# A kernel of top-k attention and two expert layers: three early expert blocks, small slots in two pieces, new priorities

## The chip, the cores and the metric

One core of a Trainium2 chip runs the whole program. The metric is the device time in microseconds of one execution. The core has five engines with a queue each: TensorE (PE; PEld is its weight load), VectorE (DVE), ScalarE (ACT), GpSimd (POOL) and SyncE (SP). Each works its queue strictly in the order in which the kernel wrote it. SyncE issues nearly all transfers, GpSimd the indirect ones.

## What is computed

Three stages follow one another. Sizes are 4 sequences of 576 tokens, 8 heads of 64, model width 512, so 2304 tokens in 18 tiles of 128.

```python
def _attn_ref(q, k, v):
    scores = scale * np.matmul(q, k.transpose(0, 1, 3, 2))
    kth = np.partition(scores, -top_k, axis=-1)[..., -top_k:-top_k + 1]   # top_k = 32
    scores = np.where(scores >= kth, scores, -1000000000.0)
    ...
    return np.matmul(attn, v)                                            # softmax over what is left

def _moe_ref(x, mu_k, mu_r, w_k, w_v, w_r):
    xk = mu_k * x + (1.0 - mu_k) * x_prev                                # x_prev: the token before
    xr = mu_r * x + (1.0 - mu_r) * x_prev
    k = np.maximum(xk @ w_k, 0.0)
    return 1.0 / (1.0 + np.exp(-(xr @ w_r))) * (k * k @ w_v)

def _moe2_ref(x, w_gate, w_local, w1, w2):                               # 8 experts, 512 -> 1024 -> 512
    for b in range(B):
        for s in range(S):
            fresh_e = int(np.argmax(logits[b, s]))
            e = fresh_e if s == 0 or local_gate[b, s] < 0.5 else prev_e
            ...
            out[b, s] = p[e] * (np.maximum(x[b, s] @ w1[e], 0.0) @ w2[e])
```

The layer in the middle has weights in 64-bit floats, which the kernel turns into 32-bit ones itself.

## The kernel before

**A planner writes the order.** Every piece of work is an `Op` of a class `Sched`: its engine, an assumed duration, what it depends on, the buffers it takes and gives back, and a priority. `Sched.run` plays the program through on these assumptions; whenever an engine is free, it takes the ready piece with the lowest priority number, and the order so found is the order of each engine's queue. To the priority that the code gives, `op` adds for each kind of work (engine and function name, as `PE minis.l1_`) a `SHIFT` and, times the number of the instance, a `SLOPE`. These tables hold about 85 kinds. The order is fixed at build time; on the chip an engine waits where its next instruction's input is late.

**Attention.** A pair (`pair`) is two heads on one tile of 128 tokens; there are 72. TensorE makes scores (L502, two heads at once on halves of the array), ScalarE copies them out (L508), VectorE finds the 32nd largest (L513 to L556), ScalarE and GpSimd mask and exponentiate (L549 to L567), TensorE transposes (L590) and multiplies with the values (L603). `keys` loads two heads' keys with four transfers (L416, L417, two for each head) into the one buffer `kn`, then TensorE transposes them (L429); `vals` loads values with four transfers (L454, L455) into five buffers; `queries` loads a tile's queries (L463).

**Middle layer.** `narrow` converts the 64-bit weights in 20 pieces (L674 to L708), from the start on. `moe` takes one or two tiles: L801 for the gate, L819 and L866 for the first product, L853 and L894 for the second, L911 and L918 for the routing's logits (L921 stores them). Its result goes to DRAM (`xd`, L905).

**Expert layer.** Tokens are gathered by expert into slots. A block "D" is 256 tokens of one expert, "S" 128, "T" 128 + 32; the small slots "T", "H", "Q" of `minis` have 32, 64 and 32 tokens. Routing (`Routing`, recorded at L1342) runs twice: early, on the first 14 tiles, which fills `KE` blocks "D" and no others, and late, on all 18, which places the rest in the fixed list `MAIN`. If a case doesn't fit the list, a general fallback runs instead. For each block `slots` loads the expert's two weight matrices (L1692, L1694; 4 MB, left out on the chip when the expert is the same as that of the block before; `kept` tells the planner where that is), splits each weight into a high and a low part (L1730 to L1735) since the product is made in three passes, gathers the tokens (L1754), transposes them (L1768), multiplies (L1792 for D and T in pieces of 12 matmuls, L1802 for S; then L1844 in pieces of 3), and scatters the result (L1312). `minis` does the same for the small slots with unsplit weights, several column groups of the array side by side (L1894 for the first product, one piece of work for each of its 4 chunks; L1910 for the second, one for each of its 8).

At the start `Sched` may fill TensorE's planned idle time with a dummy product (L1970).

Of the kernel before, what the change touches and what calls it, by code (L numbers as in the profile page):

```python
# [30 lines left out]
class Op:  # L31
    __slots__ = ("eng", "dur", "fn", "prio", "lat", "port", "mode", "new", "use", "left", "after", "ready", "end", "seq")


class Sched:


    def __init__(self, slots):

        self.cross = {"PE": 0.24, "DVE": 0.15, "ACT": 0.2, "POOL": 0.2, "SP": 0.1}  # L40
        self.same = {"PE": 0.2, "DVE": 0.1, "ACT": 0.14, "POOL": 0.14, "SP": 0.05}
        self.rel = 0.2
        self.shift, self.slope, self.scale, self.port, self.nth = {}, {}, {}, (), {}
        self.tiled, self.turn = {}, 0.1
        self.fill, self.fill_until, self.fill_dur, self.fill_tag = None, 0.0, 0.0, None
        self.free, self.loose = dict(slots), ("pb",)
        self.ops, self.count = [], {}
# [6 lines left out]
    def op(self, eng, dur, fn, deps=(), prio=0.0, new=(), use=(), lat=0.0):  # L54
        o = Op()
# [6 lines left out]
        o.mode = self.tiled.get(key, 0)  # L62
# [16 lines left out]
    def run(self):  # L79
        heads = {t: 0 for t in self.count}  # L80
# [71 lines left out]
def kernel(  # L152
# [32 lines left out]
    KE, MAIN, FULL = 2, ("DTDDDSDT", "THQTQ"), ("D" * (MB // 2) + "S" * E, "")  # L185
# [23 lines left out]
    def segs(t):  # L209
        r = []  # L210
        g = t * P
        while g < (t + 1) * P:
# [40 lines left out]
    SHIFT = {"ACT Routing.own.<lambda>": 90.83780998, "ACT keys.hi": 22.43589903, "ACT minis.fin": 1303.658946,  # L253
             "ACT minis.hev": 979.6428999, "ACT minis.rl": 274.4842701, "ACT minis.xev": -142.1804519,
             "ACT moe.ev": -371.3097322, "ACT moe.hi": 97.84617022, "ACT moe.rc": -247.9308573,
             "ACT moe.rl": 931.2484429, "ACT moe.sq": -422.5721012, "ACT narrow.hi_": -1052.938037,
             "ACT narrow.lo_": -354.1839001, "ACT narrow.o1": -255.7834887, "ACT narrow.o4b": 107.1696191,
             "ACT pair.cp": -25.34393383, "ACT pair.ev": 234.8737767, "ACT pair.ex": 630.9371884,
             "ACT pair.rl": 26.80759231, "ACT queries.hi": -127.4905844, "ACT slots.fin": -546.850338,
             "ACT slots.rl": -434.7448111, "ACT slots.thi": -335.8746519, "ACT slots.xhi": -1731.134606,  # L260
             "ACT split.hi": 1730.558906, "ACT x0_t.cs": -120.4848861, "ACT x0_t.ev": -14.27743458,
             "DVE Routing.__init__.<lambda>": 241.5412186, "DVE Routing.own.<lambda>": 252.5861327,
             "DVE Routing.place.<lambda>": 728.2549627, "DVE Routing.place.counts": 109.1720779,
             "DVE Routing.place.kinds_": 143.1441866, "DVE Routing.place.order": -146.0024522,
             "DVE Routing.place.rows": -481.6913385, "DVE Routing.place.spread": 402.3734509,
             "DVE Routing.place.tokens": -291.9940417, "DVE mix.o1": -745.2170327, "DVE mix.o2": -3353.422116,
             "DVE moe.lc": 245.0135023, "DVE moe.lo": 19.61633349, "DVE moe.xs": 357.0877612,
             "DVE narrow.o1b": -3467.233295, "DVE narrow.o2": 10.77865981, "DVE narrow.o3": 107.1405205,
             "DVE narrow.o4": 69.48365636, "DVE pair.cands": 4660.150012, "DVE pair.ch": -1353.776995,
             "DVE pair.cn": 666.4389245, "DVE pair.rx": 335.8208771, "DVE pair.th": 30.41966953,  # L270
             "DVE slots.tlo": 371.3560689, "DVE slots.xlo": -738.9035906, "DVE split.hi": 146.281663,
             "DVE split.lo": -62.01978119, "DVE kernel.ok_in": -545.3444415,
             "DVE kernel.ok_out": 95.76363139, "DVE x0_t.nrm": 1170.307626,
# [9 lines left out]
             "POOL Routing.place.<lambda>": 1917.782127, "POOL Routing.pool.consts_": 384.2200777,  # L283
             "POOL minis.gx": 351.200011, "POOL minis.sca": -202.5550864, "POOL moe.lo": 270.4878608,
             "POOL narrow.o5": 294.3819007, "POOL narrow.o5r": -298.0169726, "POOL narrow.o6": -218.326335,
             "POOL pair.nbias": 330.3710576, "POOL pair.rp": 1118.836428, "POOL pair.sp": 344.3683001,
             "POOL slots.gx": -13.98307362, "POOL slots.sca": 2858.354949, "POOL slots.tlo": -1495.820284,
             "POOL split.lo": -55.4064238, "POOL x0_t.edge": 731.5562647, "SP dma.keys": 53.35405016,
             "SP dma.queries": 14.05631517, "SP dma.raw": -1463.806281, "SP dma.small": -580.7447585,
             "SP dma.vals": -13.48047754, "SP load.go": -241.494936, "SP minis.first": 216.1179133,  # L290
             "SP minis.second": 63.77269869, "SP moe.<lambda>": 159.110049}
    SLOPE = {"ACT Routing.own.<lambda>": -1801.45762, "ACT keys.hi": 39.07940011, "ACT minis.fin": -1014.9097,
             "ACT minis.hev": 179.643281, "ACT minis.rl": -1270.934339, "ACT minis.xev": -724.8108089,
             "ACT moe.ev": 51.08183119, "ACT moe.hi": -2.29375714, "ACT moe.rc": -391.9016438,
             "ACT moe.rl": 2.954213622, "ACT moe.sq": 0.3153912355, "ACT narrow.hi_": 333.5405295,
             "ACT narrow.lo_": 990.6602289, "ACT narrow.o1": -20.67716147, "ACT narrow.o4b": -212.1268198,
             "ACT pair.cp": 1.994825142, "ACT pair.ev": -12.3860511, "ACT pair.ex": -1.136550945,
             "ACT pair.rl": 1.000926306, "ACT queries.hi": -73.7324358, "ACT slots.fin": -139.4746212,
             "ACT slots.rl": -108.2117739, "ACT slots.thi": 81.23765684, "ACT slots.xhi": 197.2386647,
             "ACT split.hi": -15.53815153, "ACT x0_t.cs": 98.06339663, "ACT x0_t.ev": -96.9242885,  # L300
             "DVE Routing.__init__.<lambda>": -5188.178896, "DVE Routing.own.<lambda>": -187.5434498,
             "DVE Routing.place.<lambda>": -33.26916612, "DVE Routing.place.counts": -1080.433612,
             "DVE Routing.place.kinds_": 1193.087661, "DVE Routing.place.order": 3085.767142,
             "DVE Routing.place.rows": -56.97482649, "DVE Routing.place.spread": 3802.902318,
             "DVE Routing.place.tokens": 181.9509213, "DVE mix.o1": -416.5312326, "DVE mix.o2": 83.38990822,
             "DVE moe.lc": 63.71582267, "DVE moe.lo": -148.0939769, "DVE moe.xs": 44.39229292,
             "DVE narrow.o1b": -8.868595585, "DVE narrow.o2": -420.7801735, "DVE narrow.o3": -245.3131375,
             "DVE narrow.o4": -45.31025859, "DVE pair.cands": -30.9391742, "DVE pair.ch": 26.82931159,
             "DVE pair.cn": 11.27550151, "DVE pair.rx": 2.99460654, "DVE pair.th": -8.218142381,
             "DVE slots.tlo": -181.6041827, "DVE slots.xlo": 283.5184965, "DVE split.hi": -49.03847711,  # L310
             "DVE split.lo": 23.23497517, "DVE kernel.ok_in": -1237.21353,
# [97 lines left out]
    def keys(b, hp, prio):  # L409
# [11 lines left out]
        for j0, nj in ((0, KJ), (KJ, 1)):  # L421
# [11 lines left out]
            def hi(pt=pt, j0=j0, w=w):  # L433
                nc.scalar.activation(kt.t[:, j0 * P:j0 * P + w], pt.t[:, :w], AF.Copy)
# [1425 lines left out]
    def minis(sc2, new, seq, T0):  # L1860
        for kind, s, je, rr_ in seq:
# [62 lines left out]
            for c in range(DC):  # L1924
                def l1_(c=c, l1=l1):
                    l1(c)
# [102 lines left out]
```

## Time and profile before

| | us |
|---|---|
| median of 3 runs | 1012.39 |
| lowest, highest | 1008.04, 1016.09 |
| the profiled execution | 1008.81 |
| its span, first to last instruction | 1007.0 |
| TensorE busy in it | 960.4 |
| VectorE busy | 803.6 |
| mean granted TensorE clock | 0.980 |

The profile's page gives busy shares of each engine over the span, the chain of work that ended last, and the costliest groups of instructions by source line. The trace behind it is asked by stretches of time (how busy each engine was in each), by waits (who waited for whom), and as a timeline. A matmul's end is modelled, so a busy TensorE may still be slower than it could be; the starts of successive pieces tell that.

### The profile page before, as it was taken

To read this page: it belongs to the slowest core of one execution; us is meant where nothing else is said; L and a number is where in the kernel's file an instruction comes from. 1 tells how busy PE (TensorE), PEld (TensorE's weight loads), DVE (VectorE), ACT (ScalarE), POOL (GpSimd) and SP (SyncE) were. 2 spreads that over 40 slices of the span, in tenths; PEclk is the share of its full clock that TensorE was granted. 3 is DMA by queue.
4 is the path that set the end of the run, shared out by engine and by line. 5 is a ranking of instruction groups with operands and counts; after the bars stand their busy time and mean duration, and the time that the engine had idled before them with its cause. 6 is when DMAs were issued, how large, how long until landed. Compare 5 with 4: busy or idle time off the path is not lost.

```text
span 1007.0 us, 22941 instructions
## 1 busy us (share of the span) xinstructions
PE 960.4 (95%) x7498; PEld 717.6 (71%) x7498; DVE 803.6 (80%) x3362; ACT 717.5 (71%) x1661; POOL 715.9 (71%) x836
## 2 busy tenths in 40 slices
PE   7889999999999999999999999999989998999995
PEld 6666666667676777777777777778677875867763
DVE  4869999998998999999768999966589775663651
ACT  5568888999896899898987988973453564544532
POOL 3658888889897899989777979973446645653531
PEclk9899999999998999999999999999899999999998
DMA  7542000121010131010010000000832999737651
GB/s 199 148 152 85 12 12 12 24 69 39 10 33 11 24 82 27 20 34 11 16 54 24 23 22 2 13 11 22 283 116 70 366 298 358 256 137 273 213 180 38
DMA packets 80596, 95.08 MB, mean 94 GB/s; under 512 B 45101, under 2 KB 49197, under 8 KB 80464
## 3 DMA queue, kind: packets, MB, share of 16 engines
q1 hardware_dynamic: 77392, 83.93, 26.3%
q0 software_dynamic: 3072, 9.57, 2.7%
q8 instruction: 61, 1.00, 0.4%
q14 instruction: 71, 0.58, 0.2%
HBM read 84.04 MB, written 9.57 MB: 93 GB/s over the span
## 4 chain that ended last, share of the span: by engine, by line
PE 55%; DVE 22%; ACT 6%; issue 5%; DMA 5%; POOL 4%; SPq 2%; DVEq 0%; POOLq 0%; ACTq 0%
PE pb L1792 7%; PE pb L502 6%; PE pv L1844 6%; PE pv L894 5%; PE pb L866 5%; PE xa L603 5%; DVE c L513 5%; PE pb L590 4%; PE pb L801 4%; DVE c L553 3%; DVE mk L544 3%; POOL mk L549 2%; DVE c L522 2%; DVE c L525 2%; PE pv L853 1%
## 5 line engine op out<-in xcount | busy, mean ns | idle before, releaser
L563 POOL TENSOR_TENSOR at<-s,at 128x576 f32<-128x576 f32 x144 | 204.1, 1427 | 26.8 <-ACT at L559 26.0
L549 POOL TENSOR_TENSOR mk<-s,mk 128x576 f32<-128x576 f32 x144 | 205.5, 1427 | 0.0
L513 DVE MAX8 c<-s 128x8 f32<-128x82 f32 (+1 forms) x1008 | 158.9, 229 | 14.9 <-ACT s L508 14.9
L502 PE MATMUL pb<-kT,qh 64*128 64x288 f32 x640 | 122.6, 460 | 7.3 <-ACT wv L708 3.2
L559 ACT ACTIVATE at<-s,TS 128x576 f32<-128x576 f32 x144 | 111.7, 777 | 22.5 <-DVE TS L556 19.0
L553 DVE MAX8 c<-mk 128x8 f32<-128x584 f32 x144 | 108.0, 756 | 19.9 <-POOL mk L549 19.9
L508 ACT ACTIVATE s<-pb 128x288 f32<-128x288 f32 (+1 forms) x320 | 115.5, 413 | 10.2 <-PE pb L502 9.1
L567 ACT ACTIVATE at<-at,sm 128x576 f32<-128x576 f32 x144 | 112.1, 780 | 12.3 <-POOL at L563 11.8
L544 DVE TENSOR_SCALAR_CACHE_REDUCE mk<-s,c 128x576 f32<-128x576 f32 x144 | 114.2, 800 | 0.0
L593 ACT ACTIVATE aT<-pb 128x384 f32<-128x384 f32 x216 | 97.2, 493 | 10.1 <-PE pb L590 9.1
L590 PE MATMUL pb<-ident,at 128*128 128x128 f32 x648 | 99.4, 282 | 4.3 <-ACT at L567 4.3
L590 PEld LDWEIGHTS pb<-ident,at 128*128 128x128 f32 x648 | 74.3, 143 | 33.5 <-ACT at L567 11.9
L894 PE MATMUL pv<-wv,kk 128*128 128x512 f32 x336 | 98.0, 417 | 0.0
L603 PE MATMUL xa<-aT,vb 128*64 128x128 f32 (+1 forms) x1600 | 94.9, 267 | 0.7 <-ACT aT L593 0.7
L603 PEld LDWEIGHTS xa<-aT,vb 128*64 128x64 f32 x1600 | 78.8, 137 | 21.3 <-issue 17.7
L866 PE MATMUL pb<-xk,wk 128*128 128x256 f32 x672 | 93.7, 291 | 0.1
L1792 PE MATMUL pb<-xk,wk 128*128 128x256 f32 x672 | 89.8, 285 | 2.0 <-DVE xk L1774 2.0
L1792 PEld LDWEIGHTS pb<-xk,wk 128*128 128x128 f32 x672 | 84.2, 188 | 9.1 <-issue 5.1
L866 PEld LDWEIGHTS pb<-xk,wk 128*128 128x128 f32 x672 | 84.9, 191 | 8.0 <-issue 2.8
L1844 PE MATMUL pv<-wv,vb 128*128 128x512 f32 x300 | 83.5, 407 | 0.0
L502 PEld LDWEIGHTS pb<-kT,qh 64*128 64x128 f32 x640 | 52.9, 189 | 40.3 <-issue 11.7
L1735 DVE TENSOR_TENSOR wk<-s,wk 128x512 fp32r<-128x512 f32 x51 | 55.7, 1114 | 28.9 <-ACT wk L1732 25.2
(266 smaller groups left out, 1955.4 us busy)
## 6 DMA issues: line engine op xcount, KB each, us to landing
s<-in_moe_w_dram SPq DMA_DIRECT2D x64, 256.0 KB, 4.7
kT<-in_moe_w_dram SPq DMA_DIRECT2D x32, 512.0 KB, 6.3
rw<-in_moe_w_dram SPq DMA_DIRECT2D x15, 512.0 KB, 6.9
at<-in_moe_w_dram SPq DMA_DIRECT2D x10, 512.0 KB, 4.8
kk<-in_moe_w_dram SPq DMA_DIRECT2D x20, 256.0 KB, 4.4
xd<-rr SPq DMA_DIRECT2D x18, 256.0 KB, 2.0
rw<-in_moe_w_k_dram SPq DMA_DIRECT2D x8, 512.0 KB, 4.6
qn<-in_q_dram SPq DMA_DIRECT2D x16, 256.0 KB, 3.0
```

What stands on the lines that cost most here:

```text
L502: nc.tensor.matmul(pcs[a].t[:, :HS], qh.t[r, hp, :], kt.t[r, c], start=True, stop=True)
L513: nc.vector.max(c8.t[:, a, c, :], s2.t[:, EDGE[c]:EDGE[c + 1]])
L544: nc.vector.tensor_scalar(mk.t[:, :S], s2.t, c8.t[:, a, NCH + 2, 7:8], 0.0, op0=OP.is_lt, op1=OP.add, accum_out=sm.t[:, 2 + a:3 + a])
L549: nc.gpsimd.tensor_tensor(mk.t[:, :S], s2.t, mk.t[:, :S], op=OP.mult)
L553: nc.vector.max(c8.t[:, a, 0, :], mk.t)
L563: nc.gpsimd.tensor_tensor(x, s2.t, x, op=OP.subtract)
L590: nc.tensor.transpose(pt.t[:, c * P:(c + 1) * P], at.t[:, (g * GB + c) * P:(g * GB + c + 1) * P], ident)
L603: nc.tensor.matmul(xa.t[a * D:(a + 1) * D, hp * P + p0:hp * P + p0 + n], vb[:, a, j, :], evs[c // GB][1].t[:, c % GB, p0:p0 + n], start=(j ...
L866: nc.tensor.matmul(pm.t[:, :N], WK[c][f // 4].t[:, x, f % 4 * P:(f % 4 + 1) * P], xk.t[:, y, c, :N], start=(m == 0), stop=(m == 3 * DC - 1))
L894: nc.tensor.matmul(pvs[ti].t, kk.t[:, x, ti * P:(ti + 1) * P], WV[f].t[:, y, :], start=(f == 0 and m == 0), stop=(f == FB - 1 and m == 2))
L1792: nc.tensor.matmul(ph.t[:, (f % 2) * N:(f % 2 + 1) * N], w[:, x], xt.t[:, y, c, :N], start=(n == 0), stop=(n == 3 * DC - 1))
L1844: nc.tensor.matmul(py.t, hT.t[:, x, o_:o_ + P], w[0].t[:, y, :], start=(f == 0 and m == 0), stop=(f == FC - 1 and m == 2))
```

## The change

It has four parts.

- `KE` is 3, not 2: the early routing fills three blocks "D". The late list has one "D" less. `kept` names the place in the list where the planner counts on no load; the last "T" no longer stands there. `b3`, the planned begin of the small slots after the blocks' begin, goes from 30 to 44.
- The small slots' two products are one piece of work each for the planner, not 4 and 8. The matmuls are the same.
- Keys are loaded with two transfers, each for both heads, not four; the planner's duration for it is halved. Loads, transposes and copies of the first sequence's keys, of its values, and those of the first queries count as kinds of their own (`keys0`, `vals0`, `queries0`, `tr0`, `hi0`).
- All `SHIFT` and `SLOPE` values are new, and two tables are added, `EARLY` and `LATE`: with m instances of a kind and h = m / 9, the n-th one's priority gets EARLY times 0.5 to the power n / h and LATE times 0.5 to the power (m - 1 - n) / h.

```diff
     def run(self):
+        for o in self.ops:
+            m = self.nth[o.key] + 1
+            h = m / 9.0
+            o.prio = o.prio + self.early.get(o.key, 0.0) * 0.5 ** (o.nth / h) + self.late.get(o.key, 0.0) * 0.5 ** ((m - 1 - o.nth) / h)
         heads = {t: 0 for t in self.count}
...
-    KE, MAIN, FULL = 2, ("DTDDDSDT", "THQTQ"), ("D" * (MB // 2) + "S" * E, "")
+    KE, MAIN, FULL = 3, ("DTDDDST", "THQTQ"), ("D" * (MB // 2) + "S" * E, "")
...
-    SHIFT = {"ACT Routing.own.<lambda>": 90.83780998, "ACT keys.hi": 22.43589903, "ACT minis.fin": 1303.658946,
...
+             "SP dma.keys": -102.4317918, "SP dma.keys0": 56.14849309, "SP dma.queries": -498.1475508,
+             "SP dma.queries0": 10.45413052, "SP dma.raw": -431.7345715, "SP dma.small": -231.7248161,
+             "SP dma.vals": 37.16374137, "SP dma.vals0": 237.2049297, "SP load.go": 106.8085623,
...
+    SLOPE = {"ACT Routing.own.<lambda>": -1610.984326, "ACT keys.hi": 21.21187526, "ACT keys.hi0": -283.5194928,
...
+             "SP dma.keys": -253.3733908, "SP dma.keys0": 1340.092052, "SP dma.queries": -34.78187054,
+             "SP dma.queries0": -1367.670809, "SP dma.raw": 131.9486322, "SP dma.small": 7669.235697,
+             "SP dma.vals": -75.45162534, "SP dma.vals0": 130.9723499, "SP load.go": 40.97117659,
...
+    EARLY = {"ACT Routing.own.<lambda>": 39.01644115, "ACT keys.hi": -284.7349795, "ACT keys.hi0": -87.75660058,
...
+             "SP dma.keys0": -64.50886934, "SP dma.queries": 126.7084932, "SP dma.queries0": 388.3107358,
...
+             "SP dma.vals0": 124.8441309, "SP load.go": 64.45799412, "SP minis.first": -708.6716305,
...
+    LATE = {"ACT Routing.own.<lambda>": -25.40150862, "ACT keys.hi": 19.0748765, "ACT keys.hi0": 99.36181289,
...
+            "SP dma.keys": 165.7459533, "SP dma.keys0": -239.0713462, "SP dma.queries": 403.0473361,
+            "SP dma.queries0": 274.283792, "SP dma.raw": 0.3699409712, "SP dma.small": -5.4936241,
+            "SP dma.vals": 420.1723432, "SP dma.vals0": -7.891970257, "SP load.go": -547.0614982,
...
-            for h in range(2):
-                e.dma_start(x[:REM, :, h, :], kk_[h, :cut].rearrange("(p j) d -> p j d", j=KJ + 1))
-                e.dma_start(x[REM:, :KJ, h, :], kk_[h, cut:].rearrange("(p j) d -> p j d", j=KJ))
-        ld = dma([go], 2.2, prio - PAR["ka"], [kn], kind="keys")
+            e.dma_start(x[:REM], kk_[:, :cut].rearrange("h (p j) d -> p j h d", j=KJ + 1))
+            e.dma_start(x[REM:, :KJ], kk_[:, cut:].rearrange("h (p j) d -> p j h d", j=KJ))
+        ld = dma([go], 1.1, prio - PAR["ka"], [kn], kind="keys" if b else "keys0")
...
-          "hp": [0, 1, 2], "ps": [0.15, 1.1], "ld": 6.2, "kept": (5, 7), "ts": [12.0, 13.7], "b2": 1650, "w0": [-20, -26],
-          "w1": [-11.5, 4.5], "g": -9.5, "l0": -61, "l1": [-14, -20], "xt": 1, "rl": 300, "l3": -40, "t3": 24.0, "b3": 30.0}
+          "hp": [0, 1, 2], "ps": [0.15, 1.1], "ld": 6.2, "kept": (5,), "ts": [12.0, 13.7], "b2": 1650, "w0": [-20, -26],
+          "w1": [-11.5, 4.5], "g": -9.5, "l0": -61, "l1": [-14, -20], "xt": 1, "rl": 300, "l3": -40, "t3": 24.0, "b3": 44.0}
...
-            for c in range(DC):
-                def l1_(c=c, l1=l1):
+
+            def l1_(l1=l1):
+                for c in range(DC):
                     l1(c)
-                o = sc2.op("PE", 2.0 * F_ / 1200, l1_, [lds[0], xo, o], T0 + 1 + 0.9 * c, [] if c else [ph, h], [xt, W1[c]] + ([ph] if c else []))
+            o = sc2.op("PE", DC * 2.0 * F_ / 1200, l1_, [lds[0], xo], T0 + 1, [ph, h], [xt, *W1])
...
-            for f in range(FC):
-                def l2_(f=f, l2=l2):
+
+            def l2_(l2=l2):
+                for f in range(FC):
                     l2(f)
-                o = sc2.op("PE", 2.0 * D_ / 1200, l2_, [lds[1], ho, o], T0 + 6 + 0.45 * f, [] if f else [py, yo],
-                           [hT, W2[max(f - 1, 0)]] + ([py] if f else []))
+            o = sc2.op("PE", FC * 2.0 * D_ / 1200, l2_, [lds[1], ho], T0 + 6, [py, yo], [hT, *W2])
```

## Rows read from the trace of the kernel before

**Rows 1.** The page's first part: busy us, share of the span, instructions.

```profile
PE 960.4 (95%) x7498; PEld 717.6 (71%) x7498; DVE 803.6 (80%) x3362; ACT 717.5 (71%) x1661; POOL 715.9 (71%) x836
```

**Rows 2.** Table of stages: stretch, length, busy us by engine, clock, DMA share, GB/s.

```profile
0.00:75.00 75.00, 63.08 (x625) 47.86 (x626) 46.73 (x166) 43.88 (x91) 37.36 (x49) 0.91 0.60 168
...
130.00:475.00 345.00, 341.22 (x2723) 246.17 (x2722) 332.31 (x1678) 303.88 (x742) 306.12 (x362) 0.99 0.11 29
475.00:696.00 221.00, 220.54 (x1757) 167.21 (x1756) 178.43 (x888) 179.91 (x437) 178.68 (x242) 1.00 0.08 21
...
735.00:773.00 38.00, 33.29 (x237) 29.17 (x236) 34.24 (x108) 16.66 (x34) 18.80 (x21) 1.00 0.19 68
773.00:838.00 65.00, 59.48 (x390) 46.89 (x386) 49.05 (x87) 35.24 (x73) 37.23 (x35) 0.99 0.94 325
...
901.00:996.00 95.00, 93.95 (x699) 64.59 (x702) 42.89 (x64) 42.23 (x89) 37.34 (x33) 1.00 0.54 183
```

**Rows 3.** TensorE's timeline in the tail: start, us, line, operands, count.

```profile
788.86 0.64 PE L1894 MATMUL pb<-rw,aT 128*32 128x256 f32 x8
...
832.40 0.64 PE L1910 MATMUL pb<-at,qh 128*32 128x128 f32 x16
832.97 0.50 PE L1844 MATMUL pv<-wv,x0T 128*128 128x512 f32 x1
...
842.15 0.42 PE L1910 MATMUL pb<-kk,qh 128*32 128x128 f32 x8
...
844.13 0.43 PE L1910 MATMUL pb<-kk,qh 128*32 128x128 f32 x8
...
994.32 0.43 PE L1910 MATMUL pb<-kk,qh 128*32 128x128 f32 x8
...
995.58 0.43 PE L1910 MATMUL pb<-kk,qh 128*32 128x128 f32 x8
```

**Rows 4.** The chain that ended last, in order of time: start, us, what.

```profile
403.28 1.44 PE pb L866 x12
...
453.16 1.63 PE pb L866 x12
...
866.06 5.76 PE pb L1792 x48
...
916.41 5.74 PE pv L1844 x24
```

**Rows 5.** The page's transfers: out<-in, queue, count, size, median us to landing.

```profile
s<-in_moe_w_dram SPq DMA_DIRECT2D x64, 256.0 KB, 4.7
```

**Rows 6.** SyncE's timeline in the tail.

```profile
737.58 3.16 SPq L1694 DMA_DIRECT2D kT<-in_moe_w_dram  x4
775.29 4.49 SPq L1692 DMA_DIRECT2D s<-in_moe_w_dram  x6
```

**Rows 7.** TensorE's waits, 735 to 838 us: total us, times, longest.

```profile
PE pv L1844 <- DVE wv L1735: 3.2, 1, 3.2
PE pb L1342 <- DVE at L1342: 2.1, 2, 1.6
PE pb L1342 <- DVE mk L1342: 1.2, 1, 1.2
PE pb L1342 <- DVE qn L1342: 1.2, 1, 1.2
```

**Rows 8.** SyncE's timeline at the start.

```profile
25.27 0.60 SPq L455 DMA_DIRECT2D vb<-in_v_dram  x1
...
26.59 0.55 SPq L416 DMA_DIRECT2D kn<-in_k_dram  x1
```

**Rows 9.** VectorE's waits, 0 to 75 us.

```profile
DVE xT L677 <- ACT xT L674: 25.5, 12, 4.4
```

**Rows 10.** TensorE's timeline at 310 us.

```profile
312.63 1.33 PE L502 MATMUL pb<-kT,qh 64*128 64x288 f32 x2 [2.45 <-DVE LG L921]
313.88 2.93 PE L866 MATMUL pb<-xk,wk 128*128 128x256 f32 x12
```

More of the change, by code (lines that the diff above doesn't have):

```diff
@@ L31 @@
 class Op:
-    __slots__ = ("eng", "dur", "fn", "prio", "lat", "port", "mode", "new", "use", "left", "after", "ready", "end", "seq")
+    __slots__ = ("eng", "dur", "fn", "prio", "lat", "port", "mode", "new", "use", "left", "after", "ready", "end", "seq", "key", "nth")
 class Sched:
@@ L43, in __init__ @@
         self.shift, self.slope, self.scale, self.port, self.nth = {}, {}, {}, (), {}
-        self.tiled, self.turn = {}, 0.1
+        self.tiled, self.turn, self.early, self.late = {}, 0.1, {}, {}
         self.fill, self.fill_until, self.fill_dur, self.fill_tag = None, 0.0, 0.0, None
@@ L61, in op @@
         o.port = eng == "POOL" or key in self.port
-        o.mode = self.tiled.get(key, 0)
+        o.mode, o.key, o.nth = self.tiled.get(key, 0), key, n
         o.eng, o.dur, o.fn, o.prio, o.lat = eng, dur * self.scale.get(key, 1.0), fn, prio, lat
@@ L252 @@
              "rr": 3, "xT": 2, "sm": 13, "rw": 3, "wk": 8, "wv": 8}
-    SHIFT = {"ACT Routing.own.<lambda>": 90.83780998, "ACT keys.hi": 22.43589903, "ACT minis.fin": 1303.658946,
[L254 to L273, printed above, removed]
[9 rows of a table removed]
[L283 to L311, printed above, removed]
-             "DVE kernel.ok_out": -11697.12776, "DVE x0_t.nrm": -292.8415581,
[9 rows of a table removed]
-             "POOL Routing.pool.consts_": 663.6215466, "POOL minis.gx": -382.7878903, "POOL minis.sca": -520.1089243,
-             "POOL moe.lo": 4.994223617, "POOL narrow.o5": -271.3119536, "POOL narrow.o5r": 77.52819072,
-             "POOL narrow.o6": 188.2468546, "POOL pair.nbias": -37.58553335, "POOL pair.rp": -12.08484048,
-             "POOL pair.sp": 2.259508359, "POOL slots.gx": 63.8901518, "POOL slots.sca": -90.03264383,
-             "POOL slots.tlo": 69.50474985, "POOL split.lo": 32.77933632, "POOL x0_t.edge": -253.4764902,
[3 rows of a table removed]
@@ L357 @@
     sc_ = Sched(SLOTS)
-    sc_.shift, sc_.slope, sc_.scale, sc_.port = SHIFT, SLOPE, SCALE, PORT
+    sc_.shift, sc_.slope, sc_.scale, sc_.port, sc_.early, sc_.late = SHIFT, SLOPE, SCALE, PORT, EARLY, LATE
     sc_.tiled = {"PE pair.mm": 1, "PE pair.avm": 2, "PE x0_t.sp": 2, "PE minis.l1_": 2, "PE minis.l2_": 2}
@@ L430, in tr @@
                     o += n
+            if not b:
+                tr.__qualname__ = "keys.<locals>.tr0"
             a = sc_.op("PE", 0.108 * nj, tr, [ld], prio - 4, [pt, kt] if j0 == 0 else [pt], [kn])
@@ L434, in hi @@
                 nc.scalar.activation(kt.t[:, j0 * P:j0 * P + w], pt.t[:, :w], AF.Copy)
+            if not b:
+                hi.__qualname__ = "keys.<locals>.hi0"
             ends.append(sc_.op("ACT", t_act(w), hi, [a], prio - 4, [], [pt, kt]))
@@ L455, in go @@
                 nc.sync.dma_start(x[hi, a, a:KJ + a, :D], v_[cut:].rearrange("(p j) d -> p j d", j=KJ))
[L456 removed]
+        VB[b, hp] = (vb, dma([go], 2.1, prio, [vb], kind="vals" if b else "vals0"))
     def queries(t, prio):
@@ L463, in go @@
                 nc.sync.dma_start(qn.t[p0:p0 + n], q[b, :, s:s + n, :].rearrange("h p d -> p h d"))
-        ld = dma([go], 1.5, prio - PAR["ka"], [qn], kind="queries")
+        ld = dma([go], 1.5, prio - PAR["ka"], [qn], kind="queries" if t else "queries0")
         qh = new("qh", [P, HP, P])
@@ L474, in hi @@
             nc.scalar.activation(qh.t.rearrange("p h x -> p (h x)"), pt.t, AF.Copy)
+        if not t:
+            tr.__qualname__, hi.__qualname__ = "queries.<locals>.tr0", "queries.<locals>.hi0"
         a = sc_.op("PE", 0.108 * HP, tr, [ld], prio - 5, [pt, qh], [qn])
```

107 lines of the change are left out of this document (106 added, 1 removed), and 66 rows, old and new, of tables (EARLY, LATE, SHIFT, SLOPE).

## The prediction

> **What bounds the kernel now.** I read the page's busy shares first, then a table of stages, then TensorE's own timeline, the chain that ended last, the waits and the transfer queue. The shares say TensorE 95%, VectorE 80%, the rest 71% [rows 1]. An average hides stages, so the next view cuts the span [rows 2]. In the first 75 us TensorE counts as 63.08 busy, but much of that is the warm-up product of L1970; VectorE works 46.73 of 75 and nothing is full. From 130 to 475 us VectorE (332.31 of 345) and TensorE (341.22) are both nearly full, from 475 to 696 TensorE alone (220.54 of 221). The expert tail follows: from 735 to 773 TensorE has 4.7 us free, from 773 to 838 5.5 us while the transfers stand at a share of 0.94, and from 901 to 996 it is busy 93.95 of 95 with VectorE at 42.89 and transfers at 0.54. So the end of the kernel is set by TensorE's order of work, and work taken off TensorE there should come off the end.
>
> What it does there shows in its timeline [rows 3]. Pieces of the small slots (L1894, L1910) sit between pieces of the large blocks (L1792, L1844): a small piece begins at 842.15, the next at 844.13, one large piece of 12 between. That pair takes 1.98 us. Without the interruption 48 matmuls of L1792 take 5.76 us, 1.44 for 12 [rows 4], and two small pieces back to back take from 832.40 to 832.97, 0.285 each [rows 3]. The interruption costs 1.98 - 1.44 - 0.285 = 0.26 us. From 994.32 to 995.58 the same with L1844: 1.26 - 0.72 (24 matmuls in 5.74 us, so 3 in 0.72 [rows 4]) - 0.285 = 0.26 us.
>
> **Small slots' products in one piece per layer.** Five small slots have 4 + 8 pieces each, 60 pieces. TensorE's timeline shows them as 49 separate visits, the first at 788.86, the last at 995.58 [rows 3]. After the change there are 10 pieces, so at most 10 visits: 39 fewer, times 0.26 = 10 us less. No matmul disappears. What may go wrong: a merged piece needs all its weights, and no longer fills a short hole. The holes are small (TensorE is free 1.05 us in 901 to 996 [rows 2]), so I take -10; the bounds are 0 (each visit filled a hole of its own price) and -10.5.
>
> Against this speaks a rule of the Trainium skill. The row says TensorE is busy 99% of 901 to 996 and its weight loads 64.59 of 95, 68% [rows 2]. Perfetto Trace Analysis, section Identifying the Most-Contended Engine, says that the matmul busy share is no good measure of nearness to the roof and that the weight loads' share is to be read instead; by that a third of TensorE is free and this term is nearly nothing, by the row it is -10. No run here shows yet which holds.
>
> **Three early expert blocks.** The early routing sees 14 of 18 token tiles and may place only double slots of 256 tokens of one expert. Routing these inputs as the reference does puts 135, 195, 12, 464, 213, 418, 332 and 23 of those tokens on experts 0 to 7: exactly three have 256, so a third early block exists (expert 6). What remains (159, 320, 12, 250, 237, 368, 160, 30) fits four doubles, one single, two 128+32 pairs and the small slots, which is the new list; the fallback does not run. Seven doubles before and after: TensorE's arithmetic is unchanged, only its place. One weight load is added: expert 6 is loaded early and again for its late remainder. Each load is 8 transfers of 256 KB and 4 of 512 KB, 4.19 MB; the page's 64 transfers of 256 KB are 8 loads [rows 5], so 9 now. It lies between the last early load, issued from 737.58, and the first late one at 775.29 [rows 6], when transfers have a share of 0.19 [rows 2]: I cost it at 0. If that cover were gone it would cost 4.19 MB at the 325 GB/s of 773 to 838, 13 us of a full queue, of which TensorE would feel part.
>
> What it gains: from 775.29 the late weights come at a full queue, and TensorE then has one more block of its own to work on. The waits of 735 to 838 are 3.2 us for weights being split (L1735), and the routing's own L1342 waits, 2.1 and 1.2 and one more of 1.2 [rows 7]. The routing chain is not shortened, so its 4.5 us stay, or move; the weight, gather and evacuation waits, 10.2 - 4.5 = 5.7, can go. I take -5, bounds -10 (all of both free stretches) and +5 (the third block's splits share VectorE, 34.24 of 38 busy in 735 to 773 [rows 2], with the routing, which so ends later).
>
> **First keys loaded apart, two issues not four.** 16 key loads drop 2 issues each, about 0.6 us apiece [rows 8]: 19 us of the transfer queue's time, nearly all of it hidden, since the queue idles for most of the attention stage. At the start it is not: the second keys are issued at 26.59, right behind the value loads of all four head pairs, whose last issue is at 25.27 [rows 8], and VectorE idles 28 us in the first 75, 25.5 of that until the first conversion step has run on ScalarE [rows 9]. Two issues less are worth 1.2 us; the second keys ahead of those 16 value issues, 16 x 0.6 = 9.6. But the new numbers rank the first queries at -105 + 10.5 + 388.3 + 274.3 = 568 (a lower number goes first), behind the first three value loads (362, 399, 512 by the same rule), 12 issues or 7 us; the second keys (56 + 1340 - 8 and two small decayed terms, 1364) still behind all four. I take -2, bounds -9.6 and +4 (some half of the 7 us).
>
> **Priorities bent at both ends.** Every kind of work gets a new offset and slope, and two terms that decay over the first and the last ninth or so of its instances. This reorders all queues, and the trace of before cannot show the result. Gain: TensorE is idle only 4.2 us from 130 to 696, so it could come only from fewer interruptions: 12 matmuls of L866 take 1.44 us undisturbed and 1.63 after another kind [rows 4]; 56 such pieces, 0.19 each, bound it at -11. Loss: one bad stall is priced at 310 us, where TensorE waited 2.45 us for L921 and then ran slowly, 12 matmuls of L866 in 2.93 us [rows 10] not 1.63; with a slow L502 on either side about 5 us for one stall. Two more bound it at +10. Between, nearer to no change because both orders come from the same planner: -2.
>
> **Sum.** Profiled execution 1008.8 (its span 1007.0 and 1.8 around it) - 10 - 5 - 2 - 2 = 989.8, so **990 us**. The runs shown lie from 1008.04 to 1016.09, the median 3.6 above the profiled one; that spread is in the range. 1% of 1012.39 is about what a measurement here can tell from no change, so faster means under 1002 and slower over 1022.
>
> **Rivals.**
> - TensorE is not what ends the tail (the skill's rule above, as a mechanism of this kernel): each small visit lies in time that would be lost to weights in transit or being split. For it: transfers are at 0.94 until 838, and an early merged piece must wait for its whole load. Against: after 901 transfers are at 0.54 and TensorE waits almost nowhere. Half or all of the 10 us goes, with the smaller of the other terms: 1008.8 - 2 to 5 - 3 = 1001 to 1004, say 1003.
> - The reordering also gives: -11 in the middle and -9.6 at the head, not -2 and -2: 990 - 9 - 7.6 = 973. For it: VectorE's 28 idle us at the start and 0.19 us per interruption. Against: both full engines of 130 to 475.
> - Slower: the new order puts products on TensorE's in-order queue whose inputs come late. Place: 130 to 696, where TensorE and VectorE are both full and a late result of one stops the other. Price: 5 us a stall, as at 310. It decides from (1022 - 990) / 5, six to seven more stalls, giving 1024. Against: before has one such stall in 566 us.
> - The third block has no tokens, or the late list does not fit: excluded by the counts above; it would run the fallback, hundreds of us.
>
> **How the numbers follow.** The forecast 0.53 (its own range 978 to 1001); TensorE not the bound 0.20, of which 0.06 is under 1002; the larger gain 0.14; stalls 0.13, of which 0.10 is over 1022. Faster 0.53 + 0.14 + 0.06 = 0.73; slower 0.10; within 1% 0.17. The range takes in the first three cases and a little of either end: 972 to 1010.
>
> **What would show it.** Right: L1894 and L1910 in ten runs, L1792 at 1.44 per 12 beside them, 901 to the end some 10 us shorter; a third early load issued between 740 and 770; TensorE's free time of 735 to 838 halved; s<-in_moe_w 72 issues. The second keys before 25 us show the head step. Wrong: TensorE's free time after 901 grows by as much as the visits saved; or 130 to 696 holds new waits over 2 us with slow matmuls behind them.

## The result, and the profile after

The changed kernel takes 982.5 us (median of 979.1 to 986.0), the kernel before, run beside it, 1010.75 us (1008.04 to 1016.09): a ratio of 0.9714, 95% interval 0.9658 to 0.9771. The forecast was 990, between 972 and 1010. The profiled execution of after took 986.0 us, the slowest of its four; that of before, 1008.8, is near the fastest of its own. So the two traces lie 23 us apart and the medians 28.

The page's first part, columns as in [rows 1]:

```profile
PE 937.8 (95%) x7508; PEld 720.6 (73%) x7508; DVE 796.0 (81%) x3361; ACT 716.0 (73%) x1661; POOL 713.7 (73%) x836
```

TensorE is busy 22.6 us less with as many matmuls (7508 records, 7498 in before), and its share stays 95%. The table of stages, cut as in [rows 2], shows where:

```profile
0.00:75.00 75.00, 60.59 (x634) 47.12 (x634) 47.81 (x161) 43.54 (x90) 35.95 (x47) 0.95 0.59 163
...
130.00:475.00 345.00, 342.73 (x2759) 248.63 (x2758) 333.02 (x1705) 309.47 (x758) 314.03 (x371) 1.00 0.11 30
475.00:696.00 221.00, 220.38 (x1763) 168.89 (x1761) 181.05 (x892) 176.71 (x429) 172.95 (x237) 1.00 0.08 22
...
735.00:773.00 38.00, 30.73 (x210) 27.58 (x208) 35.54 (x113) 20.87 (x42) 23.56 (x24) 0.97 0.46 157
773.00:838.00 65.00, 64.77 (x437) 56.26 (x438) 40.36 (x81) 30.72 (x64) 33.22 (x32) 0.97 0.85 280
838.00:901.00 63.00, 61.99 (x468) 50.15 (x467) 36.82 (x47) 35.62 (x73) 40.64 (x39) 1.00 1.00 357
```

Read the TensorE column against [rows 2]. From 773 to 838 it has 0.23 us free where it had 5.5; from 735 to 773 it has 7.3 free where it had 4.7. So the free time of 735 to 838 is 7.5 instead of 10.2 us (the sign that the forecast named was half), and two waits make up all of it, the late routing's. (The late routing runs here: the early one writes its three experts at 699.46, the late one its twelve at 761.46.) The waits for split weights, gathers and evacuations of [rows 7] are gone. TensorE's waits from 735 to 838 (us in total, times, longest):

```profile
PE pb L1439 <- DVE at L1439: 7.5, 2, 5.7
```

(The code has grown by 97 lines: L1439 is L1342 of before, L1889 is L1792, L1941 is L1844, L1991 and L2007 are the small slots' L1894 and L1910.) TensorE's timeline of the tail:

```profile
726.38 6.07 PE L1889 MATMUL pb<-xk,wk 128*128 128x256 f32 x48
732.29 0.86 PE L950 MATMUL pv<-wv,kk 128*128 128x512 f32 x3
...
773.23 1.50 PE L1439 MATMUL pb<-rw,at 128*128 128x48 bf16 x36 [5.68 <-DVE at L1439]
...
807.77 5.91 PE L1889 MATMUL pb<-xk,wk 128*128 128x256 f32 x48
...
844.75 0.65 PE L2007 MATMUL pb<-at,qh 128*32 128x128 f32 x16
845.22 1.06 PE L2007 MATMUL pb<-kk,qh 128*32 128x128 f32 x32
846.09 0.62 PE L2007 MATMUL pb<-mk,qh 128*32 128x128 f32 x16
...
886.06 5.91 PE L1889 MATMUL pb<-xk,wk 128*128 128x256 f32 x48
...
970.93 1.66 PE L1941 MATMUL pv<-wv,vb 128*128 128x512 f32 x6
```

The three rows from 844.75 are one visit: all 64 matmuls of a small slot's second layer in one go, where [rows 3] show single pieces between large ones. The whole tail has 8 visits instead of 49, the first at 824.68 where before has it at 788.86. The first row is new too: 48 products of the first expert block, 6 us of work, are done before the last piece of the middle layer, whose last matmul starts at 732.8, within 1 us of its time in before (732.0). In before the first expert product starts at 732.21. From the first expert product to the last matmul it is now 245.8 us instead of 264.0.

SyncE's timeline:

```profile
18.97 0.43 SPq L558 DMA_DIRECT2D qn<-in_q_dram  x1
...
27.20 0.63 SPq L507 DMA_DIRECT2D kn<-in_k_dram  x1
...
740.31 10.56 SPq L1789 DMA_DIRECT2D s<-in_moe_w_dram  x8
762.53 12.67 SPq L1974 DMA_DIRECT2D rw<-in_moe_w_dram  x3
```

The third early load is issued at 740.31, in the quiet stretch that the forecast named. The first load that needs the late routing's result (a small slot's) goes out at 762.53, 13 us sooner than that of before, a block's, at 775.29 [rows 6]. The second keys go out at 27.20, no earlier than the 26.59 of [rows 8]. The page's transfers show eight more of 256 KB than [rows 5], one more weight load:

```profile
s<-in_moe_w_dram SPq DMA_DIRECT2D x72, 256.0 KB, 5.2
```

### The profile page after: what moved, and what is told of

Its sections match the earlier page's. It is cut to its first block, busy times and chain, and to the rows that moved or that the text cites. A ratio compares the mean times of both kernels' runs of the same rounds, so it can differ in the third digit from the quotient of the medians.

```text
span 984.0 us, 22934 instructions
## 1 busy us (share of the span) xinstructions
PE 937.8 (95%) x7508; PEld 720.6 (73%) x7508; DVE 796.0 (81%) x3361; ACT 716.0 (73%) x1661; POOL 713.7 (73%) x836
## 4 chain that ended last, share of the span: by engine, by line
PE 55%; DVE 19%; POOL 5%; issue 5%; ACT 4%; DMA 4%; POOLq 0%; SPq 0%; DVEq 0%; ACTq 0%
PE pb L1889 6%; PE pb L599 6%; PE xa L700 6%; PE pv L991 6%; PE pb L963 6%; PE pb L898 5%; PE pv L1941 5%; PE pb L687 5%; DVE c L610 4%; DVE c L650 2%; DVE mk L641 2%; POOL mk L646 2%; PE pv L950 2%; DVE at L1439 1%; PE pb L722 1%
## 5 line engine op out<-in xcount | busy, mean ns | idle before, releaser
L664 ACT ACTIVATE at<-at,sm 128x576 f32<-128x576 f32 x144 | 111.9, 778 | 13.9 <-POOL at L660 13.5
L599 PE MATMUL pb<-kT,qh 64*128 64x288 f32 x640 | 118.4, 453 | 2.7 <-ACT qh L569 2.5
L656 ACT ACTIVATE at<-s,TS 128x576 f32<-128x576 f32 x144 | 111.4, 777 | 12.8 <-DVE TS L653 12.0
L963 PE MATMUL pb<-xk,wk 128*128 128x256 f32 x672 | 91.7, 287 | 0.0
L1889 PE MATMUL pb<-xk,wk 128*128 128x256 f32 x672 | 85.8, 283 | 1.0 <-DVE xk L1871 1.0
L1889 PEld LDWEIGHTS pb<-xk,wk 128*128 128x128 f32 x672 | 83.5, 188 | 3.8 <-DVE xk L1871 1.6
L1941 PE MATMUL pv<-wv,vb 128*128 128x512 f32 x300 | 80.6, 404 | 0.0
L599 PEld LDWEIGHTS pb<-kT,qh 64*128 64x128 f32 x640 | 51.4, 186 | 35.8 <-issue 12.8
L645 POOL TENSOR_SCALAR mk<-pick,sm 128x8 f32<-128x8 f32 x144 | 48.3, 335 | 36.7 <-DVE mk L641 25.6
```

The lines of the kernel that those rows point to most:

```text
L599: nc.tensor.matmul(pcs[a].t[:, :HS], qh.t[r, hp, :], kt.t[r, c], start=True, stop=True)
L963: nc.tensor.matmul(pm.t[:, :N], WK[c][f // 4].t[:, x, f % 4 * P:(f % 4 + 1) * P], xk.t[:, y, c, :N], start=(m == 0), stop=(m == 3 * DC - 1))
L1889: nc.tensor.matmul(ph.t[:, (f % 2) * N:(f % 2 + 1) * N], w[:, x], xt.t[:, y, c, :N], start=(n == 0), stop=(n == 3 * DC - 1))
L1941: nc.tensor.matmul(py.t, hT.t[:, x, o_:o_ + P], w[0].t[:, y, :], start=(f == 0 and m == 0), stop=(f == FC - 1 and m == 2))
```

## The experiments

The questions: which part of the change gave what; whether an interruption really costs TensorE 0.26 us (the step against the rule on weight loads); and where the new numbers, forecast at -4 us with the keys, come in. All ratios are to the kernel before, run on the same chip.

### The two structural pieces, alone and together

`m1_merge` is before with the small slots' products merged, `k1_blocks` before with the third early block, `mk_both` both; old numbers, old key loads.

```
m1, mk:  -  for c in range(DC):  o = sc2.op("PE", 2.0*F_/1200, l1_, ...)
         +  o = sc2.op("PE", DC*2.0*F_/1200, l1_, [lds[0], xo], T0 + 1, [ph, h], [xt, *W1])
         (and the same for l2_ over its 8 chunks)
k1, mk:  -  KE, MAIN = 2, "DTDDDSDT"      +  KE, MAIN = 3, "DTDDDST"
         -  "kept": (5, 7), "b3": 30.0    +  "kept": (5,), "b3": 44.0
```

> The kernel before with one edit: the small slots' two products are one piece each (10 pieces, not 60). Queues up to the tail keep their order. If TensorE's order ends the tail (the forecast): about 40 visits fewer at 0.26 us, so 10 us less, ratio 0.990, and the time between the last L853 and the last matmul falls from 264 us by as much. If visits only fill time that would be lost anyway (the rival): 0 to 3 us less, ratio 0.997 to 1.0, and TensorE's idle time in the tail grows by what the visits saved.

> The kernel before with the third early block alone (KE, MAIN, kept, b3). The forecast's step: 5 us less, ratio 0.995, from waits on weights and gathers in the 100 us after the middle layer. Rival: the third block's splits delay the late routing on VectorE and nothing is gained, 0 to 5 us more. The attention stage keeps its order and its time in both.

> Before with the merged pieces and the third block, old priorities and keys. If both steps are independent as in the forecast's sum: 15 us less, ratio 0.985. If the whole tail gain of the changed kernel (about 18 us from first block matmul to last matmul) is structure and not priorities: 18 us less, 0.982. If the two need the new priorities to be worth anything: under 8 us less.

Measured: m1_merge 0.9960 [0.9941, 0.9979], k1_blocks 0.9951 [0.9930, 0.9972], mk_both 0.9899 [0.9874, 0.9924]; in medians 1009.4 for before, then 1005.1, 1003.6 and 998.9. The two add up (4.3 + 5.8 = 10.1 against 10.5). So m1_merge lies between its two readings (10 us, and 0 to 3), k1_blocks meets the forecast's, and mk_both meets none of its three (15, 18, under 8).

Merging alone gave 4 us, not 10. Its trace has 10 visits instead of 49, so the interruptions did go, and TensorE is busy 7 us less in the tail. But its idle time there rose from 12.8 to 18.8 us, and the tail is only 1.3 us shorter (262.7 against 264.0). Its waits from 729 us on:

```profile
PE pb L1792 <- DVE xk L1774: 4.4, 1, 4.4
PE pb L1910 <- ACT qh L1905: 4.0, 2, 2.6
PE pb L1894 <- DMA at<-in_moe_w_dram: 2.7, 3, 1.3
PE pb L1894 <- DMA rw<-in_moe_w_dram: 2.1, 4, 0.7
```

The last three are the merged pieces themselves: they stand on TensorE's in-order queue until the whole load, or ScalarE's whole evacuation (L1905), is there. That took 4.0 + 2.7 + 2.1 = 8.8 us, 4.8 of it for loads; before has no waits of these three kinds, and its pieces could start on their first chunk.

The trace of k1_blocks shows another gain than the forecast's. The wait for split weights did shrink, from 3.2 to 0.2 us, but others came, and TensorE's idle time in the tail is 13.2 us against 12.8. Its order has fewer visits, however: 37 instead of 49, though no piece was merged. Its tail is 260.9 us, 3.1 shorter.

### The price of an interruption

`d1_visits` is the whole change with 50 products by zeros added between the chunks of the merged pieces. A zero product uses all 128 columns of the array, so that TensorE must leave the small slots' column groups and come back. `d0_same_mode` adds the same 50 in the small slots' own column groups. The products add zero to what is accumulated.

```
+ def zero(dst): nc.tensor.matmul(dst, ident_r[:, :64], start=False, stop=False)
  def l1_(): for c in range(DC): l1(c);  + if c < DC - 1: zero(ph)      (l2_ likewise)
d1: lhs zr (128 columns)      d0: lhs zr[:, :w] (the slot's 32 or 64)
```

> The changed kernel, and between the chunks of each small slot's two products (3 + 7 gaps, 5 slots) one product over the whole array with zero weights added to the same result: 50 more visits in the order of before, with no other work in them. If a visit costs TensorE 0.26 us and TensorE ends the tail: 13 us more than the changed kernel, ratio to before 0.984 (0.9714 + 13/1010). If visits are covered: at most 2 us more, 0.973.

> The same 50 zero products, but in the column group of the small slots themselves, so that the array's partition does not change. If the price of a visit is the change between the whole array and its column groups: 1 to 3 us more than the changed kernel (50 short instructions), ratio 0.973 to 0.975. If it is only an additional instruction that costs: the same as the run with whole-array products, 0.984.

Measured: d1_visits 0.9867 [0.9835, 0.9898], d0_same_mode 0.9756 [0.9729, 0.9783], in medians 997.1 and 984.9 us. The intervals don't touch. The ratios' difference is 1.1% of 1009 us, 11.2 us for 50 changes of mode and back: 0.22 us each. TensorE's timeline of the same slot, first d1_visits, then d0_same_mode (L2009 is the small slot's second product, L2025 the zero product):

```profile
843.88 0.43 PE L2009 MATMUL pb<-at,qh 128*32 128x128 f32 x8
844.24 0.20 PE L2025 MATMUL pb<-ident_r,zr 128*128 128x64 bf16 x1
844.38 0.43 PE L2009 MATMUL pb<-at,qh 128*32 128x128 f32 x8
844.73 0.20 PE L2025 MATMUL pb<-ident_r,zr 128*128 128x64 bf16 x1
844.87 0.42 PE L2009 MATMUL pb<-kk,qh 128*32 128x128 f32 x8
```

```profile
843.63 0.45 PE L2009 MATMUL pb<-kk,qh 128*32 128x128 f32 x8
843.85 0.19 PE L2025 MATMUL pb<-ident_r,zr 128*32 128x64 bf16 x1
843.88 0.43 PE L2009 MATMUL pb<-kk,qh 128*32 128x128 f32 x8
844.10 0.19 PE L2025 MATMUL pb<-ident_r,zr 128*32 128x64 bf16 x1
844.13 0.43 PE L2009 MATMUL pb<-kk,qh 128*32 128x128 f32 x8
```

A piece and its zero product take 0.49 us where the mode changes (843.88 to 844.38 to 844.87), and 0.25 where it doesn't (843.63 to 843.88 to 844.13): 0.24 us in the instructions themselves. It reaches the end of the kernel nearly whole: the tail is 258.9 us long in d1_visits and 248.1 in d0_same_mode, with the same idle time in it, 8.7 and 8.8. (The whole-array product also loads 128 columns of weights, not 32, so the price is that of the change of mode and of this load together.)

### The key loads

`s1_structure` is all of the change but the new numbers: mk_both with two key transfers and a planned cost of 1.1. `a_keys4` is the opposite: the whole change with four key transfers.

```
s1:       +  e.dma_start(x[:REM], kk_[:, :cut]...);  e.dma_start(x[REM:, :KJ], kk_[:, cut:]...)
          +  ld = dma([go], 1.1, ...)                 (old SHIFT and SLOPE, no kinds of their own)
a_keys4:  -  the two transfers   +  for h in range(2): the two transfers of before
```

> All that the change does but the new tables: merged pieces, third block, two key transfers with the shorter planned duration; SHIFT and SLOPE as before, no EARLY and LATE, no kinds of their own for the first loads. Forecast: 1008.8 - 10 - 5 - 1 = some 16 us less, ratio 0.984; the new tables are then worth the rest to the changed kernel, some 10 us. Rival: the tables are worth nothing, and this is at the changed kernel's 0.971.

> The changed kernel with four key transfers per load, as before; every queue's order is the changed kernel's. If the key transfers' number is nearly all hidden (forecast: 1.2 us of the start): 0 to 2 us more, ratio 0.9714 to 0.974. If the transfer queue's 19 us are felt: up to 0.990.

Measured: s1_structure 1.0161 [1.0138, 1.0185], 1025.7 us; a_keys4 0.9730 [0.9704, 0.9757], 982.7 us. Two issues less per load are worth nothing that can be measured: a_keys4 and the whole change differ by 0.2 us in medians, and their intervals overlap. But the edit under the old numbers makes the kernel 27 us slower than mk_both, where the forecast and the rival both expected it faster than before. Its tail is no worse (253.0 against 250.3 us); its first expert product comes at 759 instead of 731, with TensorE free 37.7 us before it instead of 25.2. The stage from 130 to 475, to be read against [rows 2]:

```profile
130.00:475.00 345.00, 333.54 (x2604) 238.66 (x2602) 327.35 (x1638) 295.22 (x723) 301.05 (x357) 1.00 0.11 29
```

TensorE has 11.5 us free there instead of 3.8, and VectorE 17.7 instead of 12.7. A changed planned cost of a load gave another order, and that order is worse. The largest of TensorE's waits from 130 to 760 us is for the middle layer's last rows, at 746 and 753:

```profile
PE pb L910 <- DVE rr L902: 6.4, 2, 3.4
```

What loses the rest of the 27 us stays open.

### The bent priorities

`a_no_bend` is the whole change without EARLY and LATE.

```
- sc_.early, sc_.late = EARLY, LATE      + sc_.early, sc_.late = {}, {}
```

> The changed kernel without EARLY and LATE; SHIFT and SLOPE stay the new ones, and the planner orders everything anew. If the bends carry the first and last ninths: 5 to 20 us more, ratio 0.976 to 0.991, with the loss in the first 130 us and in the tail. If they are of no account: 0.971 within 0.004. The forecast gave all new numbers together 2 us in the middle and at most 2 at the start.

Measured: 0.9769 [0.9739, 0.9798], 985.5 us, where a_keys4 on the same chip had 0.9730 [0.9704, 0.9757]. The bends are worth about 3 us by these medians; the intervals overlap, and the result lies between the two readings. The traces say more: without the bends attention's last product comes at 671.8 instead of 679.2 in after, yet the first expert product comes at 725.8 against 726.4. Seven microseconds gained in attention don't reach the expert layer.

### Which numbers pay

From mk_both to a_keys4 only the planner's numbers differ (with the first loads as kinds of their own), and 998.9 becomes 982.7: 16 us, four times what the forecast gave to numbers and keys together. `t1_tail_tables` is mk_both with new numbers for the kinds of the tail alone, `t2_front_tables` the whole change with old numbers for those kinds.

```
TAIL = ("slots.", "minis.", "Routing.", "split.", "load.")
t1: SHIFT, SLOPE, EARLY, LATE  new for kinds in TAIL, old for the others (keys as in before)
t2: SHIFT, SLOPE, EARLY, LATE  old for kinds in TAIL, new for the others
```

> Both pieces of the structure (third early block, merged small-slot products) with the old four key transfers and the old priorities for everything that attention and the middle layer issue, but with the new priorities, bends included, for the kinds of the tail (Routing, weight splits, early weight loads, expert blocks, small slots). The structure alone measured 0.990 of before and the whole change 0.971. Theory 'the new numbers pay in the tail': most of the 1.9 per cent between them comes back, 0.972 to 0.978, tail (first block product to last) 245 us, and the start of the tail stays at 730. Rival 'they pay in the stages ahead of the tail': 0.985 to 0.990, tail about 250. With both in equal parts 0.980.

> The whole change, with the tail's kinds (Routing, weight splits, early weight loads, expert blocks, small slots) put back to the old priorities and unbent; attention, middle layer and first loads keep their new numbers. Theory 'the new numbers pay in the tail': 0.982 to 0.987, with the tail back at 250 us while it still starts at about 725. Rival 'they pay ahead of the tail': 0.971 to 0.976. If the two sets depend on one another, this and the opposite mixture are both worse than halfway (over 0.981).

Measured: t1_tail_tables 0.9969 [0.9949, 0.9988], t2_front_tables 0.9898 [0.9867, 0.9929]. So the tail's numbers alone make mk_both worse by 0.7%, the others alone change nothing (0.9899 to 0.9898), and both together gain 1.7%. Neither of the two theories holds, and the third reading of the second expectation does: the sets depend on one another. The traces say how. First t1_tail_tables: the largest of TensorE's waits from 725 us on, the row of VectorE's timeline that writes the chosen experts (`es`), and the stage that holds most of the wait (columns as in [rows 2]):

```profile
PE pb L1273 <- DVE at L1273: 15.4, 2, 13.5
```

```profile
781.30 0.15 DVE L1273 CAST es<-at 1x12 int32<-1x12 f32 x1
```

```profile
778.00:792.00 14.00, 0.50 (x7) 0.21 (x6) 13.86 (x52) 5.00 (x11) 7.30 (x8) 0.63 0.50 169
```

The same row of VectorE's timeline, first in before, then in after:

```profile
773.07 0.25 DVE L1342 CAST es<-at 1x13 int32<-1x13 f32 x1
```

```profile
761.46 0.15 DVE L1439 CAST es<-at 1x12 int32<-1x12 f32 x1
```

In this mixture the middle layer's last product slips to 750 (732.8 in after), the experts are written 20 us later than in after, and TensorE, whose queue has the late routing's product next, stands 13.5 us for its input while VectorE is busy 13.86 of 14. t2_front_tables has the best start of all, its first expert product at 719.5, and gives it back in a tail of 261.0 us with 18.3 idle. Its largest waits from 690 us on (L1278 is the routing, L1728 and L1780 are the blocks' first and second product):

```profile
PE pb L1278 <- DVE at L1278: 4.3, 1, 4.3
PE pv L1780 <- POOL vb L1765: 3.7, 1, 3.7
PE pb L1728 <- DVE xk L1710: 3.6, 3, 2.0
PE pv L1780 <- ACT vb L1762: 3.3, 1, 3.3
```

### Can the routing's stall be planned away?

The largest wait left in after is the 5.68 us at 773.23. It is a wait for the late routing's rows on VectorE (the first expectation below calls them the early one's). The planner takes a step of them as 0.495 us. Such a step is two TENSOR_SCALAR; sixteen of these took 7.20 us there, which is 0.90 a step. `x1_rows_cost` tells it 0.79, `x2_rows_3pc` 0.51.

```
- "DVE Routing.place.rows": 1.5      + 2.4  (x1)      + 1.55  (x2)
```

> The whole change, with one number of the planner altered: its cost for a VectorE step of the early routing's rows goes from 0.495 to 0.79 us, since sixteen of the tensor_scalar instructions of a group took 7.20 us of VectorE with the gaps. It is meant to move the routing's transposes behind other TensorE work and take away the 5.68 us that TensorE waits at 767.5 and the low clock for 6.8 us that follows. Theory 'the planner stalls there because it thinks VectorE faster than it is': 0.964 to 0.969, stall under 2 us. Rival 'VectorE is full there (24.79 of 25 us), so a wait only moves': 0.969 to 0.975.

> The whole change with the planner's cost of the routing's rows step raised by 3 per cent (0.495 to 0.51 us) where the run before raised it by 60 per cent and came out at 0.985 instead of 0.971. A 3 per cent cost error is of no account in itself, yet the list of TensorE comes out in another order from the first expert blocks on. Theory 'the new numbers fit one order and any other list of the same work is worse by about a per cent': 0.978 to 0.986, with the stall at the routing still there or moved. Rival 'it was the wrong cost that hurt, not the other order': 0.968 to 0.975, as the whole change.

Measured: x1_rows_cost 0.9848 [0.9818, 0.9878], x2_rows_3pc 0.9802 [0.9776, 0.9828]; both worse than the whole change (0.9714; a_keys4 0.9730). The truer cost did not help: the wait shrank only to 3.85 us, the rival's range was missed as well, and the tail grew to 255.8 us. And 3% on one cost, too little to be an error of any weight, gives a TensorE order that differs in the tail, with the stall still there:

```profile
770.19 1.50 PE L1439 MATMUL pb<-rw,at 128*128 128x48 bf16 x36 [5.05 <-DVE at L1439]
```

Its tail is 253.1 us instead of 245.8, with 14.4 idle instead of 9.6. This supports the theory that the numbers fit one order, and it speaks against the rival that the changed cost itself did the harm. None of the versions run beat the changed kernel.

## Why the prediction was right, and where it was not

The sum came out at 989.8 for a profiled execution that took 986.0. The total is nearer than its parts: the structure was put 4.5 us too high, the numbers 12 us too low. These errors partly cancel, so that the total came so close is in part luck; the median, 982.5, is 7 us under the sum.

**Merged small-slot products, -10: right price, half the gain.** An interruption costs 0.22 to 0.24 us; 0.26 was forecast, and 41 visits were saved. The step that failed is "the holes are small, so I take -10". Alone the merging gave 4.3 us; beside the third block 4.7 (1003.6 to 998.9). (Between the profiled executions the second figure is larger, a tail of 250.3 us after 260.9, but mk_both's is its fastest execution.) What was given back is the cost that the forecast named and set to nothing, the wait for all inputs: 8.8 us in m1_merge, for weights and for ScalarE's evacuation. In the whole change that cost is almost gone. Of TensorE's waits from 720 us on, one row is a merged piece's:

```profile
PE pb L1991 <- DMA at<-in_moe_w_dram: 0.3, 1, 0.3
```

And d1_visits shows that there the price counts in full, 11 us for 50. This suggests that the merge pays what it promised only under an order that has its inputs ready; no run takes the merge alone out of the whole change.

**TensorE is what ends the tail: held.** The rival had the visits lie in time lost anyway. For the changed kernel d1_visits excludes it: the 50 mode changes lengthened the run by 11 us. In the kernel before it was half right: there the visits saved by m1_merge came back to a good part as idle time, 6 us of it. The table of stages of d1_visits, from 901 to 985, has TensorE at 81.56 of 84 and the weight loads at 62.01, 74% (68% in [rows 2]), so by that share a quarter of TensorE was still free:

```profile
901.00:985.00 84.00, 81.56 (x642) 62.01 (x641) 43.70 (x67) 40.71 (x85) 31.22 (x29) 1.00 0.50 177
```

The Trainium skill's page Perfetto Trace Analysis, section Identifying the Most-Contended Engine, says that the matmul busy share is no good measure of how near TensorE is to its roofline, and that MFU (the share of the peak rate of arithmetic) and the weight loads' busy share are to be used. Read as in the forecast, by the weight loads' share alone and as a sign that TensorE does not end the stage, it would have put this term near zero; the measurement decides against that use of it. The Trainium skill's page TensorEngine Tiling (Array Packing), section Tiling Modes, says that "Changing tiling mode (not just tile) drains the TensorE". The 0.49 us with and 0.25 us without a change of mode agree with it.

**Third early block, -5: right in size, by another way.** k1_blocks gave 5.8 us in medians. But in its trace TensorE doesn't wait less; twelve visits fewer, at 0.22 to 0.24 us, are 2.6 to 2.9 of the 3.1 us by which its tail is shorter. So the size was met in part by luck; the waits of 735 to 838 that the step was to remove went altogether only in the whole change. There the extra load is issued at 740.31 in quiet time, as said. The fear in the upper bound, that its splits delay the routing, didn't come true in after: the experts are written at 761.46 instead of 773.07 although VectorE is busy 35.54 of 38 there. "The routing's wait stays or moves" held: 4.5 us became 7.5.

**Keys, -2: nothing, and the stated sign was absent.** The second keys did not come before 25 us. The first queries moved from 4.47 to 18.97, behind 12 value issues, as worked out, and TensorE's first scores from 19.56 to 27.67. Neither side of this term reached the end: a_keys4 and a_no_bend, whose first queries go out at 18.69 and at 5.91, begin the expert layer at 724.9 and 725.8 (the two differ in more than their head).

**Bent priorities and new numbers, -2: mis-sized, -16.** The forecast priced the stall at 310 us [rows 10] as 5 us, and used it only to size new stalls; it did not ask whether the new order removes this one. Its removal is seen. In all five profiles with the old numbers and the old key loads ahead of the tail (before, m1_merge, k1_blocks, mk_both, t1_tail_tables) TensorE waits 2.4 to 2.5 us for the logits there, and the granted clock of 300 to 325 us is 0.86 to 0.93 (1.00 in after); in mk_both:

```profile
311.64 1.32 PE L502 MATMUL pb<-kT,qh 64*128 64x288 f32 x2 [2.45 <-DVE LG L921]
312.90 2.93 PE L866 MATMUL pb<-xk,wk 128*128 128x256 f32 x12
```

In after the longest of TensorE's waits from 130 to 696 is this one:

```profile
PE pb L898 <- DVE LG L1018: 0.6, 1, 0.6
```

That goes with the start of the tail: the first expert product is at 729.5 to 732.2 in the first four of those profiles (730.9 in t1_tail_tables) and at 723.3 to 726.6 in those with all new numbers, some 6 us earlier. The middle layer doesn't end earlier, though: its last matmul starts at 732.0 in before, 730.5 in mk_both, 732.8 in after and 731.3 in a_keys4. What is gained is the 6 us of expert work that after does before that matmul. Another 5 us are the tail's length (250.3 in mk_both, 244.9 in a_keys4), where the idle time fell from 11.9 to 8.4. The last 5 us of the 16 no profile resolves: mk_both's was its fastest execution, 4.5 us under its median, and the mean granted clock of its runs is 0.980 against 0.987 for a_keys4. That these 6 us are the stall's alone was not tested by an experiment of its own. Its absence is not enough: s1_structure has no wait of this kind either (clock 1.00 from 300 to 325), and its expert layer begins at 759.

**Rivals.** "The reordering also gives" came nearest of the three: the time lies between it and the forecast. But its places were wrong. The head gave nothing, and the middle did not gain by fewer interruptions: from 130 to 696 TensorE goes from one kind of piece to another 607 times in after and 597 times in before. "Stalls in 130 to 696" did not happen, though s1_structure shows that it can, and what it costs: 27 us from one planned cost.

## What to carry to other kernels

When a planner's order is changed, list the stalls of the old trace as gains that may fall due, not only as a price for new ones. A piece of work merged to save mode changes waits for all of its inputs, so its gain is bounded by what arrives late; look for the wait at its head. And numbers fitted to one order are worth something only together: taking half of them lost all of their gain here, and a change of one cost by 3% about half, so judge a structural edit with and without fitted numbers before calling it good or bad.

## What the runs showed of the hardware

Leaving TensorE's column groups for one whole-array product and coming back costs 0.22 us at the end of the kernel and 0.24 in the timeline, the load of 128 instead of 32 weight columns included. Two waits cost more than their length. In the stretch of the 13.5 us wait of t1_tail_tables the granted clock was 0.63, that is, part of it at the lower of the two levels (1.2 GHz), and from 792 to 796, when TensorE worked again, it was 0.58. The 2.45 us wait at 311 us was followed by twelve matmuls in 2.93 us that take 1.44 undisturbed [rows 4]. A share of 1.00 of the transfer engines for 63 us (838 to 901, 357 GB/s) did not slow TensorE: it was busy 61.99 us of it, and the 48 products at 886.06 took 5.91 us, as did 48 of L1792 in before at 759.10, in a stretch with a share of 0.19 [rows 2].
